# Two parameter loads in place of a small weight read on ScalarE's DMA queue

## The chip, the cores and the metric

The kernel runs on one core of a Trainium2 chip. The metric is the device time of one execution in microseconds (us). Of seven runs of the kernel before, the median is 180.34 us, the lowest 180.09 and the highest 180.94. The engines of the core are named as in the profile: PE (matrix multiplication, with PEld for its weight loads), DVE (vector engine), ACT (ScalarE, activations), POOL (GpSimd) and SP (which here only issues DMAs). ACT can issue DMAs, too; "ACTq" and "SPq" stand for the two issuing queues.

## The reference

The input is 2048 rows of 512 numbers. Each row is normalized; the normalized rows go through a diagonal complex state space model along the sequence and through a gated feed-forward network with a hidden width of 1376; both results are added to the input.

```python
xn = _layernorm(x, axis=-1)
return x + _A_ref(xn, ...) + _B_ref(xn, ...)

# _A_ref: state space model, 512 states
Lam = Lambda_re + 1j * Lambda_im
dt = jnp.exp(log_dt)
Lam_bar = jnp.exp(dt * Lam)
B_bar = ((Lam_bar - 1.0) / Lam)[:, None] * Bmat
Bu = jnp.einsum("bld,pd->blp", x + 0j, B_bar)
for t in range(L):
    h = Lam_bar[None, :] * h + Bu[:, t, :]
y = 2.0 * jnp.einsum("blp,dp->bld", hseq, Cmat).real + x * Dskip[None, None, :]

# _B_ref: gated network
return (silu(x @ w_gate) * (x @ w_up)) @ w_down
```

Inputs, weights and output are bfloat16.

## The kernel before

**Tiling.** The 2048 rows are 16 tiles of 128 rows (x0 to x15), in four chunks of four tiles. A chunk goes through these steps: layer norm of its tiles (statistics, L509, L527 or L479 on DVE; scale and shift into `xn_sb`), transposition of `xn_sb` into `xnT`, gate and up products (L739; for the first chunk the gate products are cut into quarters, L780), silu and copy out of PSUM on ACT (L751, L807), their product hT on DVE (L809), the state space input (L854, copied out at L861), rotation by tables, scan and rotation back on DVE (L885, L894), which leave `hss`, and the output product: `hT` with `w_down` (L937) and `hss` with `W12` (L950) into one PSUM bank, added to x on DVE (L955) and stored.

**PSUM.** Eight banks are used as four pairs. A product into a pair waits until ACT (or DVE at L955) has read what the pair held before. ACT writes the up products into two buffers `uf`, so the third waits for the hT that reads the first.

**What orders the work.** Each operation is a task with a list of tasks that it depends on and an estimated duration. PE and SP run their tasks in the order in which the code adds them. For ACT, DVE and POOL a planner (`_schedule`) walks through the estimated times and picks, among the tasks that are ready, the one with the longest estimated path behind it. For DMAs it works with an estimated bandwidth and latency of each queue. The order it makes is fixed when the kernel is built; on the chip, engines wait for each other by semaphores alone. An estimate that changes, also that of a load's arrival, can thus change the order of instructions on DVE far from the load.

**The head.** SP issues x0, x1, x2, a quarter of the first gate weights (`a2`, the last of four slices of 128 input rows), x3, three parameter loads, then the up weights, the rest of the gate weights and x4 to x7 as one load (`ld_x4`). ACT issues a small read `ld_touch` and the other three slices of the gate weights (`a0`: two slices, `a1`: one). `ld_touch` reads two numbers of each of four slices from every eighth row of the first 128 rows, into `tch`, which nothing reads. The gate weights' load `a0` keeps its place behind it through `order`. After its DMA issues ACT loads the table for Sqrt and runs one activation with it (`act_table`, L463). Then come the square roots of the first chunk (L521), each of which DVE's reciprocal (L531) waits for; the normalization (L514) follows that. PE first runs some matmuls on a constant (L474), then transposes the first normalized tiles (L565), which ACT copies out (L577).

**Parameters.** The three parameter vectors (log_dt, Lambda_im, Lambda_re) are loaded as rows of `prow`, transposed by PE (L562) together with the last tile of the first chunk and copied to `praw` (L574). From them small operations on 4 numbers per partition follow: `dt` and `r` on POOL (L636, L643), the range reductions and the complex factors on DVE (L610 to L660).

**The transposes on SP's queue.** After the head SP issues five transposing DMAs (L395): the two parts of B, `xnT` of chunk 1, and the two parts of C. Each waits for all DMAs added before it, and a plain load added after one waits for it. Behind them stand x8 to x11, `w_down` and x12 to x15. Chunk 2's statistics on DVE need x8 to x11; POOL makes `rstd` from them (L487, L491), DVE `nmr` (L500), and ACT normalizes the four tiles (L503), as it does for chunk 3.

**The scans.** A chunk has eight scans (L894), in two halves of four. A half needs its rotated input (L885) and carries a state to the next chunk.

Of the kernel before, what the change touches and what calls it, by code (L numbers as in the profile page):

```python
# [12 lines left out]
B16 = mybir.dt.bfloat16  # L13
# [236 lines left out]
def bass_parallel_sum__ssm_conv_s5__swiglu_ffn__prompt_kernel(  # L250
# [23 lines left out]
    KT = D // 128  # L274
# [6 lines left out]
    g = _Graph()  # L281
    es = ExitStack()
    with es:
        block = es.enter_context(nc.Block(no_gpsimd_drain=True))

        def sb(name, shape, dt):
            return es.enter_context(nc.sbuf_tensor(name, shape, dt))
# [41 lines left out]
        st0 = sb("st0", [128, 4, 2, 6], F32)  # L329
        sd0 = sb("sd0", [128, 4], F32)  # L330
        epst = sb("epst", [128, 1], F32)
        tch = sb("tch", [16, KT, 2], B16)
        praw = sb("praw", [128, 3, PT], B16)
        prow = sb("prow", [12, 128], B16)
        ecst = sb("ecst", [128, PT], F32)
# [1 line left out]
        NSM = 64  # L337
        sm = sb("sm", [128, NSM, PT], F32)
# [46 lines left out]
        wg_v = B_w_gate.rearrange("(k p) f -> p k f", p=128)  # L385
# [5 lines left out]
        def dma(name, dst, src, writes, nbytes, reads=(), after=(), out_=False, eng="sp", xpose=False, prio=0.0, order=(), **kw):  # L391
            after = tuple(after)
            if xpose:
                after = after + tuple(dma_tasks)
                fn = lambda e, dst=dst, src=src: e.dma_start_transpose(out=dst, in_=src)  # L395
                est, nb = 2000.0, int(nbytes * 1.2)
            else:
                if xp_state[0] is not None:
                    after = after + (xp_state[0],)
                fn = lambda e, dst=dst, src=src: e.dma_start(dst, src, **kw)  # L400
                est, nb = 330.0 + nbytes / 900.0, nbytes
            t = g.add(eng, fn, reads=reads, writes=writes, name=name, dma=True, after=after, out=out_, est=est, nbytes=nb, prio=prio, order=order)
            dma_tasks.append(t)
            if xpose:
                xp_state[0] = t
            return t
# [6 lines left out]
        def pload(name, slot, src, **kw):  # L413
            return dma(name, prow[4 * slot:4 * slot + 4, :], src.rearrange("(a p) -> a p", p=128), [("prow", slot)], 1024, **kw)

        def x_load(a, **kw):
            return dma("ld_x%d" % a, x_sb[:, a:a + 1, :], x_v[:, a:a + 1, :], [("x", a)], TILEB, **kw)

        def wg_load(nm, k0, k1, **kw):
            return dma("ld_wg" + nm, wg[:, k0:k1, 0:FG], wg_v[:, k0:k1, 0:FG], [("wg", nm)], (k1 - k0) * 128 * FG * 2, **kw)  # L420

        x_load(0)
        x_load(1)
        act_q = [dma("ld_touch", tch[0:16], wg_v[0:128:8, :, 0:2], [("tch",)], 16 * 16, eng="act")]
        act_q.append(wg_load("a0", 0, 2, eng="act", order=(act_q[-1],)))
        x_load(2)
        act_q.append(wg_load("a1", 2, 3, eng="act", order=(act_q[-1],)))
        wg_load("a2", 3, 4)
        x_load(3)
        pload("ld_ldt", 2, A_log_dt)  # L430
        pload("ld_lim", 1, A_Lambda_im)
        pload("ld_lre", 0, A_Lambda_re)
        dma("ld_wu0", wu[:, :, 0:FH0], wu_v[:, :, 0:FH0], [("wu", 0)], 512 * FH0 * 2)
        dma("ld_wg1", wg[:, :, FG:Fh], wg_v[:, :, FG:Fh], [("wg", 1)], 512 * (Fh - FG) * 2)
# [7 lines left out]
        def loads_stage_b2():  # L442
# [13 lines left out]
              reads=[("ones",)], writes=[("ident",)], name="ident", est=300)  # L456
        g.add("pool", lambda e: e.iota(iot[:], pattern=[[1, TP]], base=0, channel_multiplier=0, allow_small_or_imprecise_dtypes=True),
              writes=[("iot",)], name="iota", est=1000)
# [1 line left out]
        g.add("pool", lambda e: e.memset(car[:, 0], 0.0), writes=[("car", 0, 0), ("car", 0, 1)], name="car0", est=100)  # L460
        g.add("pool", lambda e: e.memset(ecst[:], math.e), writes=[("ecst",)], name="ecst", est=100)
        def act_table(func, order):
            g.add("act", lambda e: e.activation(out=sm[:, NSM - 1, 0:1], in_=epst[:], func=func, bias=epst[:, 0:1]), reads=[("epst",)], writes=[("sm", "_warm")],  # L463
                  name="act_warm", est=1500, order=order)

        act_table(AF.Sqrt, (act_q[-1],))

        def pe_warm(n, w=512, bk=None):
# [292 lines left out]
        def ffn_gate_quarters(pairs):  # L761
# [27 lines left out]
            for a_, b_ in zip(seq, seq[1:]):  # L789
                hold[b_].od.add(hold[a_])  # L790
            act_table(AF.Silu, (hold["ev21"],))
            hold["evac"] = g.tasks[-1]
            ffn_mm(0, NQ, "g", xt_pair[0])
# [275 lines left out]
```

## Time and profile before

| | |
|---|---|
| median of 7 runs | 180.34 us (180.09 to 180.94) |
| the profiled execution | 180.35 us |
| its span in the profile | 178.6 us |
| PE busy | 174.4 us (98%) |
| DVE busy | 162.2 us (91%) |
| ACT busy | 88.7 us (50%) |
| granted PE clock | 1.00 in the whole span |
| DMA | 12.37 MB, of it 11.54 MB on SP's queue and 0.69 MB on ACT's |

The span begins with the first instruction that the profile sees and ends with the last; the rest of the execution's time lies around it. PE's busy time has to be read with care, since matmuls are pipelined and overlap in the records: a row of the timeline that says 379 ns for a matmul stands for a new matmul every 216 ns. A timeline row gives start and duration in us, engine, line, operation, output and inputs; in brackets stands how long the engine had been idle before it and what ended that. In the chain of waits a row gives start, duration and what the end of the execution waited for in that stretch.

The landing times of the head's loads, from issue: x0 2.3 us, x1 3.0, x2 3.7, x3 4.3, `ld_touch` 2.1, a0 3.8, a1 4.3 and a2 4.4. The transposes land after 4.2 to 4.6 us, but that of chunk 1's `xnT` after 6.0.

### The profile page before, as it was taken

How to read it: one execution, taken by the hardware profiler on the slowest of the kernel's cores; microseconds unless marked ns; L12 is line 12 of the kernel's file. 1: busy time of each engine (PE TensorE's matmuls, PEld its weight loads, DVE VectorE, ACT ScalarE, POOL GpSimd, SP SyncE). 2: the span in 40 equal slices, each digit the busy share in tenths (PEclk: the TensorE clock that was granted, in tenths of full speed). 3: DMA queues.
4: the chain of work that ended last, by engine and by line, in shares of the span. 5: the costliest groups of instructions: out<-in, count | busy, mean ns of one | idle time of the engine just before them, and what ended most of it. 6: DMA issues, size and time to landing. Idle time of an engine off the chain costs nothing.

```text
span 178.6 us, 2429 instructions
## 1 busy us (share of the span) xinstructions
PE 174.4 (98%) x937; PEld 83.9 (47%) x937; DVE 162.2 (91%) x281; ACT 88.7 (50%) x114; POOL 9.5 (5%) x21
## 2 busy tenths in 40 slices
PE   8899999999999999999999999999999999999994
PEld 2794444444434444444444444444444444444743
DVE  2958984888899999999999999999999999999983
ACT  4469999999699957016565651000965620000000
POOL 3023200001300000040000000000000000000000
PEclk9999999999999999999999999999999999999999
DMA  5995563669360000002330000001100000000122
GB/s 165 386 319 119 117 121 43 129 174 352 118 117 4 0 0 0 0 6 86 84 65 0 0 0 4 0 0 59 59 0 4 0 0 0 0 0 4 59 88 89
DMA packets 22978, 12.37 MB, mean 69 GB/s; under 512 B 15192, under 2 KB 22968, under 8 KB 22968
## 3 DMA queue, kind: packets, MB, share of 16 engines
q1 hardware_dynamic: 22472, 11.54, 23.7%
q10 hardware_dynamic: 496, 0.69, 1.1%
q8 instruction: 7, 0.11, 0.3%
q14 instruction: 3, 0.02, 0.1%
HBM read 6.46 MB, written 2.10 MB: 48 GB/s over the span
## 4 chain that ended last, share of the span: by engine, by line
PE 94%; DMA 2%; ACT 2%; DVE 1%; issue 0%; SPq 0%
PE pb L739 34%; PE pb L937 21%; PE pb L950 16%; PE pb L854 15%; PE pb L780 4%; PE pb L817 2%; DMA x_sb<-in_A_x_dram 2%; PE pb L827 1%; PE pb L565 1%; ACT xn_sb L503 1%; ACT uf L807 1%; DVE st L509 0%; SPq L400 0%; ACT xnT L577 0%; DVE xn_sb L514 0%
## 5 line engine op out<-in xcount | busy, mean ns | idle before, releaser
L894 DVE TENSOR_TENSOR_SCAN rot<-sm,car,rot 128x512 bf16<-128x512 f32 x32 | 39.0, 1266 | 0.1
L937 PE MATMUL pb<-wd,hT 128*128 128x512 bf16 (+3 forms) x198 | 38.8, 355 | 0.0
L739 PE MATMUL pb<-xnT,wu 128*128 128x512 bf16 x160 | 37.3, 379 | 0.3 <-ACT uf L807 0.3
L739 PE MATMUL pb<-xnT,wg 128*128 128x512 bf16 x132 | 31.3, 379 | 0.0
L950 PE MATMUL pb<-W,hss 128*128 128x512 bf16 (+2 forms) x144 | 28.3, 355 | 0.0
L854 PE MATMUL pb<-xnT,BT 128*128 128x512 bf16 x128 | 28.1, 379 | 0.0
L937 PEld LDWEIGHTS pb<-wd,hT 128*128 128x128 bf16 (+1 forms) x198 | 18.5, 98 | 19.9
L739 PEld LDWEIGHTS pb<-xnT,wu 128*128 128x128 bf16 x160 | 15.5, 98 | 19.5 <-ACT uf L807 0.8
L751 ACT ACTIVATE sg<-pb 128x1024 bf16<-128x1024 f32 x20 | 20.1, 1025 | 8.5 <-PE pb L739 7.4
L807 ACT ACTIVATE uf<-pb 128x1024 bf16<-128x1024 f32 x20 | 20.6, 1028 | 6.8 <-PE pb L739 5.9
L950 PEld LDWEIGHTS pb<-W,hss 128*128 128x128 bf16 x144 | 13.5, 98 | 14.3
L739 PEld LDWEIGHTS pb<-xnT,wg 128*128 128x128 bf16 x132 | 12.7, 98 | 15.7 <-issue 0.8
L854 PEld LDWEIGHTS pb<-xnT,BT 128*128 128x128 bf16 x128 | 12.5, 98 | 15.1
L861 ACT ACTIVATE u_sb<-pb 128x1024 bf16<-128x1024 f32 x16 | 16.4, 1026 | 4.4 <-PE pb L854 4.1
L809 DVE TENSOR_TENSOR hT<-sg,uf 128x1024 bf16<-128x1024 bf16 x20 | 13.4, 680 | 1.1 <-ACT uf L807 1.0
L885 DVE TENSOR_TENSOR rot<-u_sb,cosT 128x2048 bf16<-128x2048 bf16 x8 | 9.7, 1217 | 2.8 <-ACT cosT L700 2.8
L955 DVE TENSOR_TENSOR x_sb<-pb,x_sb 128x512 bf16<-128x512 f32 (+2 forms) x18 | 10.9, 623 | 1.4 <-PE pb L950 1.4
L503 ACT ACTIVATE xn_sb<-x_sb,nmr,rstd 128x512 bf16<-128x512 bf16 x8 | 5.9, 804 | 9.9 <-DVE nmr L500 9.9
L836 ACT ACTIVATE sg<-pb 96x1024 bf16<-96x1024 f32 x2 | 2.0, 1019 | 17.3 <-PE pb L817 17.3
L885 DVE TENSOR_TENSOR rot<-rot,cosT 128x2048 bf16<-128x2048 bf16 x8 | 9.7, 1217 | 0.1
L885 DVE TENSOR_TENSOR rot<-rot,sin 128x2048 bf16<-128x2048 bf16 x8 | 9.7, 1218 | 0.0
L885 DVE TENSOR_TENSOR rot<-u_sb,sin 128x2048 bf16<-128x2048 bf16 x8 | 9.7, 1214 | 0.0
(78 smaller groups left out, 142.5 us busy)
## 6 DMA issues: line engine op xcount, KB each, us to landing
out_dram<-x_sb SPq DMA_DIRECT2D x15, 128.0 KB, 1.7
x_sb<-in_A_x_dram SPq DMA_DIRECT2D x3, 512.0 KB, 7.4
wd<-in_B_w_down_dram SPq DMA_DIRECT2D x1, 1280.0 KB, 6.9
wu<-in_B_w_up_dram SPq DMA_DIRECT2D x1, 768.0 KB, 4.8
wu<-in_B_w_up_dram SPq DMA_DIRECT2D x1, 608.0 KB, 7.0
x_sb<-in_A_x_dram SPq DMA_DIRECT2D x4, 128.0 KB, 3.4
wg<-in_B_w_gate_dram SPq DMA_DIRECT2D x1, 480.0 KB, 5.9
wg<-in_B_w_gate_dram ACTq DMA_DIRECT2D x1, 448.0 KB, 3.8
```

The source lines that it names most:

```text
L503: g.add("act", lambda e, a=a: e.activation(out=xn_sb[:, a % NXN, :], in_=x_sb[:, a, :], func=AF.Identity, scale=rstd[:, a:a + 1], bias=nmr ...
L739: inst = e.matmul(pbank[0:fs, bk, :].rearrange("p (j t) -> p j t", j=4), lhsT=w[:, kt, i * 128:i * 128 + fs], rhs=xnT[:, c % 2, :, kt, :], ...
L751: g.add("act", lambda e: e.activation(out=sg[rows, sl, 0:n, :].rearrange("p a t -> p (a t)"), in_=pair_f32(rows, bk, 512 * n), func=AF.Sil ...
L807: g.add("act", lambda e: e.activation(out=uf[rows, ul, 0:n, :].rearrange("p a t -> p (a t)"), in_=pair_f32(rows, bk, 512 * n), func=AF.Ide ...
L809: g.add("dve", lambda e: e.tensor_tensor(out=hT[rows, hb, i0:i0 + n, :], in0=sg[rows, sl, 0:n, :], in1=uf[rows, ul, 0:n, :], op=ALU.mult), ...
L854: inst = e.matmul(pbank[:, bk, :].rearrange("p (j t) -> p j t", j=4), lhsT=BT[:, ri, kt, pt * 128:(pt + 1) * 128], rhs=xnT[:, c % 2, :, kt ...
L861: g.add("act", lambda e: e.activation(out=u_sb[:, us].rearrange("p r t -> p (r t)"), in_=pair_f32(slice(0, 128), b0), func=AF.Identity), r ...
L885: tt = lambda out, a, b, op, r, w, nm: g.add("dve", lambda e: e.tensor_tensor(out=out, in0=a, in1=b, op=op), reads=r, writes=w, name="%s_% ...
L894: g.add("dve", lambda e, A0=A0, A1=A1, k=k, ri=ri, pt=pt: e.tensor_tensor_scan(out=A1[:, k, ri, :], data0=rr[:, pt:pt + 1].to_broadcast([1 ...
L937: inst = e.matmul(pbank[:, bk, 0:nc_], lhsT=hT[0:fs, hb, i, lt * 128:(lt + 1) * 128], rhs=wd[0:fs, i, c0:c0 + nc_], start=(i == 0), stop=F ...
L950: inst = e.matmul(pbank[:, bk, 0:nc_], lhsT=hss[:, hb, pt, ri, lt * 128:(lt + 1) * 128], rhs=W12[:, ri, pt, c0:c0 + nc_], start=False, sto ...
L955: g.add("dve", lambda e, bk=bk, a=a, c0=c0, nc_=nc_: e.tensor_tensor(out=x_sb[:, a, c0:c0 + nc_], in0=pbank[:, bk, 0:nc_], in1=x_sb[:, a, ...
```

## The change

On ACT's queue `ld_touch` and its tile `tch` go; the loads of log_dt and Lambda_im, which were on SP's queue, are issued there, in this order, ahead of a0. On SP's queue only Lambda_re is left of the three. The activation that comes with a table load loses its bias operand.

```diff
-        tch = sb("tch", [16, KT, 2], B16)
...
-        act_q = [dma("ld_touch", tch[0:16], wg_v[0:128:8, :, 0:2], [("tch",)], 16 * 16, eng="act")]
+        act_q = [pload("ld_ldt", 2, A_log_dt, eng="act")]
+        act_q.append(pload("ld_lim", 1, A_Lambda_im, eng="act", order=(act_q[-1],)))
         act_q.append(wg_load("a0", 0, 2, eng="act", order=(act_q[-1],)))
         x_load(2)
         act_q.append(wg_load("a1", 2, 3, eng="act", order=(act_q[-1],)))
         wg_load("a2", 3, 4)
         x_load(3)
-        pload("ld_ldt", 2, A_log_dt)
-        pload("ld_lim", 1, A_Lambda_im)
         pload("ld_lre", 0, A_Lambda_re)
...
-            g.add("act", lambda e: e.activation(out=sm[:, NSM - 1, 0:1], in_=epst[:], func=func, bias=epst[:, 0:1]), reads=[("epst",)], writes=[("sm", "_warm")],
+            g.add("act", lambda e: e.activation(out=sm[:, NSM - 1, 0:1], in_=epst[:], func=func), reads=[("epst",)], writes=[("sm", "_warm")],
```

As built, PE and POOL have the same instructions in the same order as before, and ACT's order differs only in its DMA issues. DVE's order differs in three places, shown here as built, other rows left out:

```diff
 L574 TensorCopy praw<-pb 128x12
-L651 TensorCopy sm<-praw 128x4 x2
-L610 TensorTensor sm<-sm 128x4 x3
-L660 Reciprocal sm<-sm 128x4
 L479 BNStats st<-x_sb 128x6 x4
 L483 BNStatsAggregate mv<-st 128x2 x4
...
 L622 TensorScalarPtr sm<-sm 128x4
+L651 TensorCopy sm<-praw 128x4 x2
+L610 TensorTensor sm<-sm 128x4 x3
+L660 Reciprocal sm<-sm 128x4
...
 L885 TensorTensor rot<-rot 128x2048
-L894 TensorScalarPtr rot<-sm,car,rot 128x512
 L479 BNStats st<-x_sb 128x6 x4
...
 L894 TensorScalarPtr rot<-sm,car,rot 128x512
 L500 TensorScalarPtr nmr<-mv,rstd 128x4
+L894 TensorScalarPtr rot<-sm,car,rot 128x512
 L843 TensorTensor hT<-sg,uf 96x2x512
...
 L903 TensorCopy ctmp<-rot 128x2x2
-L955 TensorTensor x_sb<-pb,x_sb 128x512
+L885 TensorTensor rot<-u_sb,cosT 128x2048
+L955 TensorTensor x_sb<-pb,x_sb 128x512 x2
 L500 TensorScalarPtr nmr<-mv,rstd 128x4
-L885 TensorTensor rot<-u_sb,cosT 128x2048
-L955 TensorTensor x_sb<-pb,x_sb 128x512
 L885 TensorTensor rot<-u_sb,sin 128x2048
```

In the first of these places the four normalizations of tiles 4 to 7 (L495) also stand ahead of the first hT (L809) instead of behind it. Line numbers are those of the kernel before; in the changed kernel lines from 332 on are one lower, and from 463 on two lower.

## The prediction

> **What bounds the kernel now.** I read the chain of waits first. It says 94% PE; in order of time PE runs from 6.44 us to 176.27 us with one stop. Then I read the end of the chain, and the timelines of DVE and of SP's queue for what sets that stop and how close DVE is behind PE.
>
> ```profile
> 48.12 1.41 ACT xn_sb L503 x2
> 49.53 0.92 ACT uf L807
> 50.45 0.05 issue
> 50.49 8.81 PE pb L739 x40
> ...
> 159.73 9.58 PE pb L937 x66
> 169.30 6.96 PE pb L950 x48
> ```
>
> The stop: L739 starts at 50.49 us, after 0.33 us of idle PE, because ACT normalized four tiles (L503) before it emptied the PSUM pair that PE wanted (L807). ACT had waited for nmr (L500) on DVE, and nmr goes back to a load:
>
> ```profile
> 38.23 1.28 DVE L894 TENSOR_TENSOR_SCAN rot<-sm,car,rot 128x512 bf16<-128x512 f32 x1
> 40.94 2.47 DVE L479 BATCH_NORM_STATS2 st<-x_sb 128x6 f32<-128x512 bf16 x4 [1.42 <-DMA x_sb<-in_A_x_dram]
> ...
> 46.32 0.16 DVE L500 SCALAR_TENSOR_TENSOR nmr<-mv,rstd 128x4 f32<-128x4 f32 x1 [0.86 <-POOL rstd L491]
> 46.40 0.68 DVE L843 TENSOR_TENSOR hT<-sg,uf 96x1024 bf16<-96x1024 bf16 x1
> 47.00 2.45 DVE L894 TENSOR_TENSOR_SCAN rot<-sm,car,rot 128x512 bf16<-128x512 f32 x2
> ...
> 79.64 0.16 DVE L500 SCALAR_TENSOR_TENSOR nmr<-mv,rstd 128x4 f32<-128x4 f32 x1 [0.26 <-POOL rstd L491]
> ...
> 166.28 2.36 DVE L885 TENSOR_TENSOR hss<-rot 128x2048 bf16<-128x2048 bf16 x2
> ```
>
> Note the brackets (idle time before the row and what ended it): 1.42 us until x tiles 8 to 11 landed, 0.86 us on POOL, 0.26 us at 79.64. After that the DVE rows follow each other without an idle bracket up to 170.94. The last row writes the last hss, which ends at 168.64; the first weight load of the matmuls that read it (L950) is at 169.08 in the weight-load timeline. With a hop of 0.05 (L807 ends 50.44, PE starts 50.49) DVE has 169.08 - 168.64 - 0.05 = 0.39 us in hand there. So two chains run to the end: PE's, pinned at 50.49, and DVE's, pinned at 40.94, only 0.39 us shorter. Both hang on one transfer, issued here:
>
> ```profile
> 13.83 2.29 SPq L395 DMA_TRANSPOSE BT<-in_A_B_re_dram  x1
> 18.17 2.07 SPq L395 DMA_TRANSPOSE BT<-in_A_B_im_dram  x1
> 22.52 1.80 SPq L395 DMA_TRANSPOSE xnT<-xn_sb  x1
> 28.55 1.97 SPq L395 DMA_TRANSPOSE hss<-in_A_C_re_dram  x1
> 33.17 1.86 SPq L395 DMA_TRANSPOSE hss<-in_A_C_im_dram  x1
> 37.42 0.37 SPq L400 DMA_DIRECT2D x_sb<-in_A_x_dram  x1
> ```
>
> Each waits for the one before to land; the first waits for all loads of the head, the last of which is x4 to 7 (DVE waited for it until 13.61).
>
> **The change, part by part.**
>
> SP's queue loses the rows log_dt (3.13 us) and Lambda_im (3.55); Lambda_re stood at 3.85. So that load and the four behind it are issued 3.85 - 3.13 = 0.72 us earlier. Does x4 land earlier? The windows table says what limits it:
>
> ```profile
> 11.50:12.00 0.50, 0.50 (x10) 0.38 (x7) 0.00 (x0) 0.49 (x2) 0.00 (x0) 1.00 1.10 368
> 12.00:12.50 0.50, 0.50 (x12) 0.50 (x10) 0.35 (x2) 0.14 (x1) 0.27 (x1) 1.00 1.11 352
> ```
>
> The next to last column is the DMA engines' share: it is 0.99 or more in every half microsecond from 3.0 to 13.0. The engines set the landing, not the issue, and the bytes are the same but for 64 four-byte packets. Bounds: 0.72 us earlier if issue decided after all; 0.30 us later if the engines lost all of the time by which the first gate weights are issued later (next part). I take 0: before 3.0 us ScalarE's queue moved 15.4% in 2.4 to 3.0, so 0.30 us of it is 0.05, and the removed packets (9.1% of 0.4 us) give 0.04 back.
>
> ScalarE's queue: log_dt (0.38 by SP's row) takes the place of the weight read (0.41), and Lambda_im adds SP's spacing 3.85 - 3.55 = 0.30. So a0 and a1 are issued at 1.53 and 2.02 instead of 1.23 and 1.72, and all behind them on ACT moves: table load 2.23 to 2.53, warm activation 3.53 to 3.83, ending at 4.12. The first Sqrt (sd0) started at 4.02 on mv; it may start some 0.1 late and end at 4.4. Its reader, the reciprocal L531, starts at 4.65, held by the half statistics of tile 1 (L509 at 4.31, x1 landing at 4.29), so 0.2 us of cover is left. a0 lands 1.23 + 3.8 = 5.03, would land 5.33, and is wanted at 6.44; a1 at 6.3 for 7.33. x1 may even land earlier, since a0 shared the engines with its last packets (ScalarE's queue has 83 to 97% of the engines from 3.0 to 4.2, SP's 7 to 18%); then sd0 is next, so the gain ends near 4.65 - 4.45 = 0.20. Head: -0.20 to +0.10. It costs or gives nothing at the end, because PE only reaches the stop at 50.16 earlier or later and starts again at 50.49 all the same; without that cover it would count whole.
>
> [...]
>
> Bounds for a0 without the read ahead, by the rows: the read took 2.1 us to land and a0 3.8. If a0 now paid those 2.1 us on top, it would land at 5.33 + 2.1 = 7.4, 1.0 us late, of which the stop hides 0.33: a loss of 0.7 us at most. At the other end it lands as before after its issue. I take 0, since the parameter loads, too, come ahead of it on that queue, and 1.1 us is in hand.
>
> The removed bias of the warm activation changes one operand, no instruction. POOL and PE keep their order.
>
> DVE's order changes. In the order as built, the six parameter operations (two casts, three multiplies, reciprocal; 12.54 to 13.40, 0.85 us) move from ahead of the statistics of tiles 4 to 7 to behind them. They lay under the wait for x4, so DVE now idles and does them after 17.0. xn4 to 7 (L495) now stand ahead of the first hT: 17.0 + 0.85 + 0.1 = 17.95, ending 19.24; hT 17.87 becomes 19.24. Behind the late hT waits uf of 19.82 on ACT (two buffers), now 19.9; ACT then had 0.33 us of idle before 21.48. DVE's 2.81 us of idle before 31.78 hides the rest. Cost 0.
>
> The scan at 38.23 moves behind nmr. Before it filled the wait for the load; now that wait is longer and the scan comes at 46.40, ahead of L843. One scan by spacing: (64.94 - 60.09)/4 = 1.21 and 9.42/8 = 1.18 (150.00 to 159.42), say 1.19. Queued behind it is all of DVE: L843 47.59, the two scans 48.19, hT at 51.8 and so on. Who waits: the uf activations (54.18 on ACT needs 52.4: free), PE's first L950 (75.30 needs W at 73.73 + 1.19 = 74.92: 0.38 left). At 79.64 the second nmr is also moved, behind a 1.13 us product and one addition; so POOL's rstd is ready in time and the gap there (78.70 + 0.60 = 79.30 to 79.64) closes: 0.34 given back, at the price of ACT's L503 at 82.4 and its first silu at 85.3 instead of 84.39, taken up by ACT's 0.70 gaps. What remains is 1.19 - 0.34 = 0.85, and with no idle row it reaches 166.28. The last hss is then done at 168.64 + 0.85 = 169.49, its weights load at 169.54 instead of 169.08: PE stops 0.46 us, and the additions and stores behind it end as much later.
>
> Sum, against the profiled execution (180.35 us; its span 178.6 and 1.75 around it; the runs' median is 180.34): 180.35 + 0.46 = 180.8.
>
> **The rivals.** Let e be how much earlier x8 to 11 land. PE can come at most 0.33 (the stop) plus 0.20 (head) earlier; DVE's end moves by 0.46 - e. The change is the larger of -min(e, 0.53) and 0.46 - e.
>
> Faster: the transpose at 22.52 took 6.0 us where the other two of its line took 4.3. Its last packets lie behind one instruction read of 0.02 MB at 26.3 to 27.0. If they escape it, e = 1.7, the stop goes, the late scan costs nothing: 180.35 - 0.53 = 179.8. It decides from e = 0.46 on, where the change is nothing; from e = 0.82 on the gain is over 0.36. For it: the collision is by a hair. Against: the read follows PE's place, and a PE that is earlier meets more of the transfer.
>
> No difference: e of 0.1 to 0.8, from the 0.72 us of issue time, or a DVE chain with idle too small to be shown: at e = 0.72 it is 180.35 - 0.26 = 180.1, at 0.46 it is 180.35. Against it stands the DMA share.
>
> Slower still: x4 lands 0.30 later and all of the transposes with it; both pins move, 180.8 + 0.3 = 181.1. Or a0 is late by the bound of 0.7 past the stop; then PE, not DVE, sets the end: 180.35 + 0.7 = 181.05. For it: a0 and its queue are the only loads that the change delays. Against: a0 has 1.1 us in hand (5.33 against 6.44).
>
> That the change does not do what it says is no rival here: each engine's order is fixed when the kernel is built.
>
> **How the numbers follow.** Forecast (180.6 to 181.0) 0.52, faster 0.25, no difference 0.13, slower still 0.10. A change of 0.2% is 0.36 us, about what a measurement of this kernel can tell from none. Of the forecast's 0.52 some 0.07 falls under 180.70, so slower 0.45 + 0.10 = 0.55, same 0.20, faster 0.25. The range reaches from the faster case (179.8, a little under) to just past slower still: 179.75 to 181.2; the forecast's own range is 180.6 to 181.0.
>
> **What would show it.** Right: DVE's statistics of tiles 8 to 11 start near 40.9 after about 2.6 us of idle, a scan directly behind nmr, no idle at the second nmr, and an idle PE of near 0.46 us released by DVE before the last L950. Wrong: the gap between the third and fourth transpose near 4.3 us instead of 6.0, a first transpose more than 0.3 us from 13.83, idle DVE rows between 47 and 166, or first L780 matmuls that wait for wg.

## The result, and the profile after

| | before | changed |
|---|---|---|
| median | 180.28 us (179.80 to 180.99, 31 runs) | 181.51 us (181.02 to 182.12, 12 runs) |
| ratio, 95% interval | | 1.0068 [1.0055, 1.0081] |
| profiled execution (span) | 180.35 us (178.6) | 181.44 us (179.7) |
| PE, DVE, ACT busy | 174.4, 162.2, 88.7 us | 175.0, 161.6, 87.8 us |

The change makes the kernel slower by 0.68%, or some 1.2 us; between the two profiled executions it is 1.1 us. The forecast was slower by 0.46 us. The granted clock is 1.00 in both. Line numbers of the changed kernel are one or two lower than before (L477 is L479 before, L892 is L894, L948 is L950).

The chain of waits of the changed kernel, which was 94% PE before (start, duration, what the end waited for):

```profile
by line: DVE rot L883 23.5%; DVE rot L892 20.5%; DMA x_sb<-in_A_x_dram 7.3%; DVE hT L807 6.0%; DVE hss L883 5.1%; DVE st L477 4.1%; PE pb L948 4.0%; DVE x_sb L953 3.3%; DMA xnT<-xn_sb 3.2%; DMA hss<-in_A_C_im_dram 2.4%; DMA hss<-in_A_C_re_d
...
23.54 5.72 DMA xnT<-xn_sb
29.29 4.20 DMA hss<-in_A_C_re_dram
33.51 4.36 DMA hss<-in_A_C_im_dram
37.88 3.65 DMA x_sb<-in_A_x_dram
41.55 2.48 DVE st L477 x4
45.05 1.87 POOL rstd L489
47.17 1.20 DVE rot L892
...
167.91 2.28 DVE hss L883 x2
170.24 7.13 PE pb L948 x48
```

The end now hangs on DVE, from the landing of x8 to 11 (37.88 + 3.65 us) to the last `hss`; PE has only the last row. The timelines of PE, DVE and SP's queue of the changed kernel give the sizes:

```profile
51.15 1.04 PE L737 MATMUL pb<-xnT,wu 128*128 128x512 bf16 x4 [1.22 <-ACT uf L805]
...
170.24 5.14 PE L948 MATMUL pb<-W,hss 128*128 128x512 bf16 x23 [0.28 <-DVE hss L883]
...
41.55 2.48 DVE L477 BATCH_NORM_STATS2 st<-x_sb 128x6 f32<-128x512 bf16 x4 [3.60 <-DMA x_sb<-in_A_x_dram]
...
47.01 0.16 DVE L498 SCALAR_TENSOR_TENSOR nmr<-mv,rstd 128x4 f32<-128x4 f32 x1 [0.93 <-POOL rstd L489]
47.09 1.28 DVE L892 TENSOR_TENSOR_SCAN rot<-sm,car,rot 128x512 bf16<-128x512 f32 x1
...
82.92 0.15 DVE L498 SCALAR_TENSOR_TENSOR nmr<-mv,rstd 128x4 f32<-128x4 f32 x1
...
167.83 2.34 DVE L883 TENSOR_TENSOR hss<-rot 128x2048 bf16<-128x2048 bf16 x2
...
14.88 1.97 SPq L394 DMA_TRANSPOSE BT<-in_A_B_re_dram  x1
...
37.88 0.37 SPq L399 DMA_DIRECT2D x_sb<-in_A_x_dram  x1
```

Against the rows shown of before: the first transpose is issued 1.05 us later (13.83, now 14.88). On the way the transposes give back more than half: x8 to 11 are issued 0.46 later (37.42, 37.88). They land 0.61 later (L477 starts at 41.55 instead of 40.94), `nmr` comes 0.69 later (46.32, 47.01) and the last `hss` 1.55 later (166.28, 167.83). PE, which reached its stop earlier than before (51.15 - 1.22 = 49.93, before 50.16), goes on 0.66 later (50.49, 51.15), and a second stop, 0.28 us of shown idle, has come at the last L948.

Why the first transpose is late shows in part in the windows table. The last three columns are granted clock, the DMA engines' busy share and GB/s. First the changed kernel:

```profile
2.50:3.00 0.50, 0.50 (x3) 0.22 (x2) 0.00 (x0) 0.33 (x1) 0.00 (x0) 1.00 1.20 288
3.00:3.50 0.50, 0.50 (x3) 0.21 (x2) 0.49 (x1) 0.50 (x1) 0.00 (x0) 1.00 0.79 83
3.50:4.00 0.50, 0.50 (x3) 0.15 (x1) 0.47 (x3) 0.49 (x2) 0.00 (x0) 1.00 0.71 242
...
6.50:7.00 0.50, 0.50 (x13) 0.50 (x10) 0.47 (x3) 0.20 (x1) 0.00 (x0) 1.00 1.06 251
7.00:7.50 0.50, 0.50 (x13) 0.50 (x10) 0.50 (x3) 0.29 (x2) 0.00 (x0) 1.00 0.86 273
7.50:8.00 0.50, 0.50 (x13) 0.50 (x10) 0.42 (x2) 0.28 (x2) 0.00 (x0) 1.00 0.98 338
```

and the same stretches of the kernel before:

```profile
2.50:3.00 0.50, 0.50 (x3) 0.22 (x2) 0.00 (x0) 0.50 (x1) 0.00 (x0) 1.00 0.74 169
3.00:3.50 0.50, 0.50 (x3) 0.21 (x2) 0.42 (x1) 0.50 (x1) 0.00 (x0) 1.00 1.01 287
3.50:4.00 0.50, 0.50 (x3) 0.15 (x1) 0.45 (x2) 0.31 (x2) 0.00 (x0) 1.00 1.02 383
...
6.50:7.00 0.50, 0.50 (x12) 0.50 (x10) 0.50 (x2) 0.36 (x1) 0.00 (x0) 1.00 1.06 395
7.00:7.50 0.50, 0.50 (x12) 0.50 (x10) 0.47 (x4) 0.13 (x1) 0.00 (x0) 1.00 1.06 393
7.50:8.00 0.50, 0.50 (x13) 0.50 (x10) 0.44 (x3) 0.44 (x2) 0.00 (x0) 1.00 1.08 406
```

There are two dips. The one at 3.0 to 4.0 us loses (287 - 83 + 383 - 242) x 0.5 us = 172 KB, the one at 6.5 to 8.0 loses (395 - 251 + 393 - 273 + 406 - 338) x 0.5 us = 166 KB; at some 390 GB/s these are 0.44 and 0.43 us. Other stretches give part of it back. From 2.5 to 3.0 the changed kernel moves more than before (288 against 169 GB/s), so that by 4.0 us it is 124 KB behind in all, 0.32 us at the same rate; it gains again after 8.0 us, and at 13.0 it is 209 KB behind, 0.54 us. The rest of the 1.05 lies in the end of these loads, which thins out: 297, 115 and 14 GB/s in the three half microseconds from 13.0 to 14.5, where before only the first still moved anything, at 12 GB/s. Why it does is not shown. In the row 6.50:7.00 the engines are as busy as before (1.06) and move 251 GB/s instead of 395: the busy share is no measure of what is moved.

### The profile page after: what moved, and what is told of

Read it like the earlier page. It is cut to its first block, busy times and chain, and to the rows that moved or that the text cites. A ratio compares the mean times of both kernels' runs of the same rounds, so it can differ in the third digit from the quotient of the medians.

```text
span 179.7 us, 2428 instructions
## 1 busy us (share of the span) xinstructions
PE 175.0 (97%) x937; PEld 84.1 (47%) x937; DVE 161.6 (90%) x281; ACT 87.8 (49%) x114; POOL 10.7 (6%) x21
## 4 chain that ended last, share of the span: by engine, by line
DVE 74%; DMA 15%; PE 4%; SPq 2%; POOL 1%; issue 1%; DVEq 0%
DVE rot L883 24%; DVE rot L892 20%; DMA x_sb<-in_A_x_dram 7%; DVE hT L807 6%; DVE hss L883 5%; DVE st L477 4%; PE pb L948 4%; DVE x_sb L953 3%; DMA xnT<-xn_sb 3%; DMA hss<-in_A_C_im_dram 2%; DMA hss<-in_A_C_re_dram 2%; SPq L399 2%; DVE xn_sb L587 2%; DVE W L712 1%; DVE W L709 1%; DVE x_sb L589 1%
## 5 line engine op out<-in xcount | busy, mean ns | idle before, releaser
L892 DVE TENSOR_TENSOR_SCAN rot<-sm,car,rot 128x512 bf16<-128x512 f32 x32 | 39.0, 1266 | 0.0
L948 PE MATMUL pb<-W,hss 128*128 128x512 bf16 (+2 forms) x144 | 28.3, 355 | 0.3 <-DVE hss L883 0.3
L948 PEld LDWEIGHTS pb<-W,hss 128*128 128x128 bf16 x144 | 13.4, 98 | 14.7 <-DVE hss L883 0.5
L477 DVE BATCH_NORM_STATS2 st<-x_sb 128x6 f32<-128x512 bf16 x12 | 7.4, 682 | 6.0 <-DMA x_sb<-in_A_x_dram 6.0
```

Source lines behind the costliest of these rows:

```text
L477: return g.add("dve", lambda e, a=a: e.bn_stats(out=st[:, a, :], in_=x_sb[:, a, :]), reads=[("x", a)], writes=[("st", a)], name="bnst%d" % ...
L892: g.add("dve", lambda e, A0=A0, A1=A1, k=k, ri=ri, pt=pt: e.tensor_tensor_scan(out=A1[:, k, ri, :], data0=rr[:, pt:pt + 1].to_broadcast([1 ...
L948: inst = e.matmul(pbank[:, bk, 0:nc_], lhsT=hss[:, hb, pt, ri, lt * 128:(lt + 1) * 128], rhs=W12[:, ri, pt, c0:c0 + nc_], start=False, sto ...
```

## The experiments

The planner's order depends on the loads, so in most experiments the order of DVE and ACT was given by lists taken from the kernel before or from the changed one:

```diff
+        for eng_, order_ in (("dve", DVE_ORDER), ("act", ACT_ORDER)):
+            ts_ = [t for t in g.tasks if t.eng == eng_ and not t.dma]
+            streams[eng_] = [t for t in streams[eng_] if t.dma] + [ts_[i] for i in order_]
```

"Order before" and "changed order" mean these lists; ACT's list is the same in both. The kernel before was measured beside each group, with medians of 180.75, 180.51 and 180.50 us, so ratios are compared, not times.

**The two halves of the change.** First only the order: the kernel before and its loads, with the changed order on DVE.

> The loads of the kernel before, with DVE's order of the changed kernel. If the order costs what the prediction said (one scan, less the gap at the second nmr, less 0.39 us in hand), the end is 0.4 to 0.5 us later: 180.7 us, a stop of PE of about 0.45 us before the last L950, first transpose near 13.8 us. If the order costs nothing by itself and only late transfers do: 180.3 us.

Measured: ratio 1.0020 [1.0005, 1.0036]. Its timelines of PE and DVE:

```profile
50.67 1.90 PE L741 MATMUL pb<-xnT,wu 128*128 128x512 bf16 x8 [0.50 <-ACT uf L809]
169.70 5.57 PE L952 MATMUL pb<-W,hss 128*128 128x512 bf16 x26 [0.22 <-DVE hss L887]
...
41.11 2.47 DVE L481 BATCH_NORM_STATS2 st<-x_sb 128x6 f32<-128x512 bf16 x4 [2.91 <-DMA x_sb<-in_A_x_dram]
...
46.50 0.16 DVE L502 SCALAR_TENSOR_TENSOR nmr<-mv,rstd 128x4 f32<-128x4 f32 x1 [0.87 <-POOL rstd L493]
...
167.30 2.35 DVE L887 TENSOR_TENSOR hss<-rot 128x2048 bf16<-128x2048 bf16 x2
```

The second stop is there without any change of the loads, released by DVE's last `hss`. From `nmr` to the last `hss` DVE takes 167.30 - 46.50 = 120.80 us, before 166.28 - 46.32 = 119.96: the order adds 0.84, where the prediction said 0.85. The loss, 0.0020 x 180.75 = 0.36 us (0.09 to 0.65 by its interval), is close to the forecast's 0.46 for this part.

Then only the loads: the changed kernel with the order before.

> The loads of the changed kernel, with DVE's order of the kernel before. If the loads alone move the transposes, the first of them starts near 14.9 us, x8 to 11 land 0.6 us later, the stop ends near 51.1 and the time is 0.6 to 0.7 us above before: 180.95 us, with no stop before the last L950. If the order is all: 180.3 us.

Measured: 1.0018 [1.0003, 1.0034]. Its windows and its only stop of PE:

```profile
3.00:3.50 0.50, 0.50 (x3) 0.21 (x2) 0.50 (x1) 0.50 (x1) 0.00 (x0) 1.00 0.95 95
3.50:4.00 0.50, 0.50 (x3) 0.15 (x1) 0.47 (x3) 0.49 (x2) 0.00 (x0) 1.00 0.64 191
...
50.85 1.90 PE L739 MATMUL pb<-xnT,wu 128*128 128x512 bf16 x8 [0.64 <-ACT uf L807]
```

The first dip comes with the loads, the second does not (380, 341 and 387 GB/s from 6.5 to 8.0), and the first transpose starts at 14.49. x8 to 11 land 0.32 later than before (DVE's statistics at 41.26), PE goes on 0.36 later, and no stop follows at the end. So each half costs about 0.2%, and one does it through DVE's end, the other through PE's stop.

**The changed kernel once more**, beside the second group.

> The changed kernel once more, beside the others on one chip: if its loss is the sum of late loads (0.33 us measured alone) and late scan (0.36 us measured alone), 0.7 us above before; if the two add to more, 1.2 us as in the first measurement.

Measured: 1.0070 [1.0045, 1.0096], with both dips (117 GB/s in 3.0 to 3.5, 264 in 7.0 to 7.5) and both stops (2.00 at 52.10, 0.25 at 171.16). The whole measures more than the two halves (0.20% + 0.18%). Taken with the first measurement, 0.68%, the surplus is 0.30%, just clear of an uncertainty of 0.26% that the three intervals give together; with this second one alone it would not be. In the profiles the difference is the second dip, which neither half shows, and a chunk-1 transpose of 6.33 us.

**Is it the missing read ahead?** The changed kernel with the small read put back ahead of the two parameter loads, changed order.

```diff
-        act_q = [pload("ld_ldt", 2, A_log_dt, eng="act")]
+        act_q = [dma("ld_touch", tch[0:16], wg_v[0:128:8, :, 0:2], [("tch",)], 16 * 16, eng="act")]
+        act_q.append(pload("ld_ldt", 2, A_log_dt, eng="act", order=(act_q[-1],)))
```

> The changed kernel with the small read of the gate weights put back ahead of the two parameter loads on ACT's queue, DVE's order of the changed kernel. Theory of the read ahead: the slow first packets of the gate weights go, x4 to 7 land near 13.6 us again and only the order is left to pay: 180.7 us. Theory of the queues (parameter loads ahead of a0 on ACT's queue and earlier issue on SP's spoil the transfers): x4 to 7 land at 14.6 us or later: 181.5 us.

Measured: 1.0089 [1.0057, 1.0121], no better than without it (1.0068 and 1.0070). a0 is issued at 2.13 us, the dip lasts to 4.5 (157, 195, 190 GB/s), and x8 to 11 land at 42.41. The theory of the read ahead falls: with the read, the dip stays. But a0 is issued later still here, so this run alone does not part the read from the time of issue; the next three do.

**Is it the read alone that matters?** The kernel before without the small read, parameters on SP, order before.

```diff
-        act_q = [dma("ld_touch", tch[0:16], wg_v[0:128:8, :, 0:2], [("tch",)], 16 * 16, eng="act")]
-        act_q.append(wg_load("a0", 0, 2, eng="act", order=(act_q[-1],)))
+        act_q = [wg_load("a0", 0, 2, eng="act")]
```

> The kernel before without the small read; parameter loads stay on SP's queue, DVE's order of before. Theory of the read ahead: first packets of a0 take some 0.25 us each as in the changed kernel, x4 to 7 land about 1 us later, 180.95 us. Theory of the queues: as before or a little faster, since a0 is issued 0.44 us earlier: 180.0 to 180.3 us.

Measured: 1.0046 [1.0026, 1.0067]. There is no dip (375, 390 GB/s), but with a0 issued at 0.79, beside x0, the first x tiles land later: the first statistics, of x0, start at 3.48 us instead of 3.08, those of x1 at 5.03 instead of 4.31. PE is idle ahead of its first transposes, and its first gate products then run at half speed:

```profile
5.96 0.40 PE L565 MATMUL pb<-ident,xn_sb 128*128 128x128 bf16 x2 [0.92 <-DVE xn_sb L514]
...
7.02 1.70 PE L780 MATMUL pb<-xnT,wg 128*128 128x128 bf16 x14
8.51 0.42 PE L565 MATMUL pb<-ident,xn_sb 128*128 128x128 bf16 x2
8.72 1.40 PE L780 MATMUL pb<-xnT,wg 128*128 128x128 bf16 x14
```

From 7.02 to 8.72 these are 16 matmuls, 14 gate products and two transposes, 106 ns each. In the kernel before the same 16 take 6.28 to 7.17, 56 ns each:

```profile
6.28 0.94 PE L780 MATMUL pb<-xnT,wg 128*128 128x128 bf16 x14
...
7.17 0.94 PE L780 MATMUL pb<-xnT,wg 128*128 128x128 bf16 x14
```

So the small read has a use: with it a0 is issued at 1.23 instead of 0.79, and the statistics of x0 and x1 start 0.40 and 0.72 us earlier. In these runs the weights came too early as well as too late: a0 at 0.79 went with 0.46% more time, a0 at 1.67, in the kernel with the loads only, with 0.18%.

**What makes the dip?** Two kernels with the order before. In the first a second small read, of other rows, delays a0, and the parameters stay on SP. In the second one parameter load takes the small read's place.

```diff
+        act_q.append(dma("ld_touch2", tch2[0:16], wg_v[4:128:8, :, 0:2], [("tch2",)], 16 * 16, eng="act", order=(act_q[-1],)))
```

> The kernel before with a second small read of the gate weights (16 rows, 64 packets) between the first and a0, so that a0 is issued near 1.67 us as in the changed kernel, but with no parameter load ahead of it; parameters on SP's queue, DVE's order of before. If the later issue of a0 makes the slow packets from 3.0 to 3.75 us: the same dip (below 200 GB/s there), x4 to 7 near 14.3 us, time 0.3 us above before. If it is the parameter loads ahead of a0: no dip, x4 to 7 near 13.7 us, time as before.

```diff
-        act_q = [dma("ld_touch", tch[0:16], wg_v[0:128:8, :, 0:2], [("tch",)], 16 * 16, eng="act")]
+        act_q = [pload("ld_ldt", 2, A_log_dt, eng="act")]
...
-        pload("ld_ldt", 2, A_log_dt)
```

> The kernel before with log_dt in the place of the small read (a0 issued near 1.4 us, close to the 1.23 of before), the other parameters on SP's queue, DVE's order of before. If a parameter load ahead of a0 makes the slow packets by its form (4 rows, 4 packets): a dip below 200 GB/s between 2.7 and 3.75 us, x4 to 7 near 14.1 us. If the time of a0's issue does: hardly a dip, x4 to 7 near 13.7 us, time as before.

Measured: 1.0018 [0.9999, 1.0037] and 1.0020 [1.0001, 1.0039]. The times do not tell the two apart, the transfers do. The issue of a0 on ScalarE's queue and the windows, first of the kernel with two small reads:

```profile
1.71 0.97 ACTq L403 DMA_DIRECT2D wg<-in_B_w_gate_dram  x2
...
3.00:3.50 0.50, 0.50 (x3) 0.21 (x2) 0.39 (x1) 0.50 (x1) 0.00 (x0) 1.00 0.80 154
```

then of the one with one parameter load:

```profile
1.38 0.92 ACTq L401 DMA_DIRECT2D wg<-in_B_w_gate_dram  x2
...
3.00:3.50 0.50, 0.50 (x3) 0.21 (x2) 0.46 (x1) 0.50 (x1) 0.00 (x0) 1.00 0.98 281
```

The first has no parameter load on ScalarE's queue and dips; the second has one and does not. What goes with the dip is the time at which a0 is issued: 1.66 us and later dips at 3.0 to 3.5, 1.38 and earlier does not, in all profiles of this case. What the dip costs is not shown by this pair: the kernel without it is as slow as the one with it, and its first transpose starts at 14.20, against 14.31 with the dip and 13.83 before.

**The parameter loads behind the weights**: small read, a0 and a1 as before, then the two parameter loads on ScalarE's queue, order before.

```diff
         act_q.append(wg_load("a1", 2, 3, eng="act", order=(act_q[-1],)))
+        act_q.append(pload("ld_ldt", 2, A_log_dt, eng="act", order=(act_q[-1],)))
+        act_q.append(pload("ld_lim", 1, A_Lambda_im, eng="act", order=(act_q[-1],)))
```

> The kernel before with log_dt and Lambda_im on ACT's queue, but behind a0 and a1, the small read ahead of a0 kept; DVE's order of before. If the parameter loads spoil the transfers only by standing ahead of a0: no dip from 3.0 to 3.75 us and x4 to 7 near 13.6 us or earlier, time as before (the table load comes 0.7 us later, of which 0.2 us in the head have cover and 0.33 us the stop hides: 0 to 0.2 us more). If any parameter load on ACT's queue, or the earlier issue on SP's queue, is enough: x4 to 7 at 14.3 us, time 0.3 us above before.

Measured: 1.0053 [1.0034, 1.0072], a median of 181.39 us over six runs. There is no dip (352, 382 GB/s), but ACT's table load moves to 3.15 and its first Sqrt to 4.65, so that the first normalized tile is late. The profiled execution, with 180.25 us the lowest of the six, has no stop at 50 and does not show what the others lost; of this kernel only the transfers are read.

**Is it a0's place behind x2?** The changed kernel with x2 issued behind a2 on SP's queue, changed order.

```diff
-        x_load(2)
         act_q.append(wg_load("a1", 2, 3, eng="act", order=(act_q[-1],)))
         wg_load("a2", 3, 4)
+        x_load(2)
```

> The changed kernel with x2 issued behind the last slice of the first gate weights instead of ahead of it, changed order on DVE. Theory A (the slow first transfers between 3 and 4 us come from the first gate weights being issued after x2, whose transfer then comes first on the engines): the dip (83 GB/s in 3.0 to 3.5) goes, to 280 GB/s or more, the first transpose starts near 13.9 instead of 14.88 and the time falls to about 180.8 (the late scan alone is left), unless x2 itself is late for its statistics and costs the head 0.2 us or more. Theory B (they come from the time of issue alone, 1.67 us and later): the dip stays, the first transpose stays at 14.5 or later, the time near 181.5.

Measured: 1.0053 [1.0030, 1.0076]. The dip stays, deeper (72 and 118 GB/s), so theory A falls. x2 lands late as the expectation allowed: its statistics start at 7.55 after 1.83 us of idle, and PE stops 1.03 us in the head, which sets the end here. Why a late a0 starts slowly stays open.

**Does everything hang on x8 to 11?** Both kernels with the load of x8 to 11 issued ahead of the two transposes of C, each with its own DVE order.

```diff
+            dma("ld_x8", x_sb[:, 8:12, :], x_v[:, 8:12, :], [("x", a) for a in range(8, 12)], 4 * TILEB)
...
-            dma("ld_x8", x_sb[:, 8:12, :], x_v[:, 8:12, :], [("x", a) for a in range(8, 12)], 4 * TILEB)
```

> The kernel before, with the load of x8 to 11 issued ahead of the two transposes of C instead of behind them, engine orders as before. Theory (the end hangs on the landing of x8 to 11, by two chains): the statistics of tiles 8 to 11 have no DMA wait any more (it was 1.42 us), the stop of PE near 50.5 (0.33) goes, and the time falls by 0.33 us to about 180.0. Rival (the two transposes of C, now later by one load of about 4 us, become the next thing that is late, or PE loses in the stage at another place): the stop goes but the time does not fall, 180.3 or more.

> The changed kernel with the same early load of x8 to 11, with the changed order on DVE. Theory (the whole loss of about 1.2 us is the late landing of x8 to 11, once through PE's stop near 51 and once through the late scan): both PE's stop near 51 (1.22) and the one before the last output product (0.28) go, and the time is that of the kernel before with the same early load, within 0.3 us, near 180.0 or below, since PE had reached its stop 0.23 us earlier in the changed kernel (49.93 against 50.16). Rival (part of the loss is in the head, in the slower first transfers themselves): it stays 0.5 us or more above its counterpart.

Measured: 0.9966 [0.9949, 0.9982] for the kernel before, 0.9959 [0.9942, 0.9977] for the changed one (179.79 and 179.76 us). For the kernel before that is 0.61 us, where 0.33 was forecast; in its profile 0.22 us more is there at the first gate product already (6.06 against 6.28), and counts now that no stop follows. The second kernel, from its windows, its DVE timeline and the chain on its page:

```profile
3.00:3.50 0.50, 0.50 (x3) 0.22 (x2) 0.50 (x1) 0.50 (x1) 0.00 (x0) 1.00 0.72 132
3.50:4.00 0.50, 0.50 (x3) 0.15 (x1) 0.47 (x3) 0.49 (x2) 0.00 (x0) 1.00 0.85 270
...
37.75 2.47 DVE L479 BATCH_NORM_STATS2 st<-x_sb 128x6 f32<-128x512 bf16 x4
...
164.82 2.35 DVE L885 TENSOR_TENSOR hss<-rot 128x2048 bf16<-128x2048 bf16 x2
...
PE 96%; ACT 1%; ACTq 1%; DVE 0%; issue 0%
```

The first dip and the late scan are still there, the statistics wait for no DMA, no stop of PE is left after 45 us, and the loss of 0.68% is gone. This settles the path: neither the first dip nor the late scan costs time once x8 to 11 land early.

Last, the kernel before with the early load and the planner's own order.

> The kernel before with the early load of x8 to 11, with the planner's own orders, which that earlier landing changes on DVE and ACT. Theory (the landing decides): no stop of PE near 50.5, about 180.0. Rival (the new order brings a wait of its own, as the changed kernel's order did): a stop of PE between 50 and the end with another releaser than the normalization of tiles 8 to 11, 180.3 or more.

Measured: 0.9970 [0.9952, 0.9988]. The new order brings no stop. Three kernels thus beat the kernel before by 0.3 to 0.4%, and the changed one by more; their intervals do not tell them apart.

## Why the prediction was right and wrong

**The direction and the late scan: right.** The step "0.85 lag less 0.39 in hand" held: `nmr` is 0.69 late, the last `hss` 1.55, so 0.86 was added in between (0.84 with the order alone), and the gap at the second `nmr` closed (no bracket at 82.92). The order alone measured 0.36 us where the step said 0.46.

**The step that failed** is the landing of x4 to 7: "I take 0", with a bound of 0.30 us on the late side. DVE's wait for it ended at 14.72 us instead of 13.61, and the first transpose was issued 1.05 us late, of which 0.61 reached the landing of x8 to 11 and moved both chains, PE's by 0.66 and DVE's by 0.69. The sum with the measured term is 0.46 + 0.66 = 1.12, against 1.1 between the profiles. The mechanism is that of the rival "slower still"; its 0.30 was too small. Two readings led there. A busy share of 0.99 was taken for full transfer, but 0.95 goes with 95 GB/s in the kernel with the loads only. And the 0 took a0's delay at the 15.4% that ScalarE's queue moved before 3.0 us, 0.05 us, where by 4.0 us the transfers were 0.32 us behind. That is near the bound, whose own base was short: it took log_dt's issue at SP's 0.38 us, but on ScalarE it lasts 0.55, and a0 came at 1.67, 0.44 later and not 0.30. No term stood for the second dip and for the thin end of the loads. The kernel with the loads only, which has no second dip, shows 0.32 of the 0.61 at the landing of x8 to 11; what brings the rest stays open.

**The head: right.** The first gate product starts at 6.12 instead of 6.28, and PE reached its stop 0.23 earlier, just past the bound of 0.20, which gave nothing, as said. a0 was in time: no gate product waits for it. The six parameter operations cost nothing: PE has no idle bracket between 8 and 49.9 us.

**The faster rival did not happen.** The chunk-1 transpose did not escape the instruction reads: it took 5.72 us, against 6.03 before, with two reads in it. That the read follows PE's place is seen later in the execution: the last four of the seven larger reads come behind 451, 579, 707 and 834 recorded matmuls in both profiles. In this transpose the larger read came behind 196 matmuls, at 24.50 us, where before it came behind 204, at 26.50.

## What to carry to other kernels

Read the GB/s column beside the busy share before a transfer is called limited by its engines (a share of 1.06 stood beside 251 GB/s and beside 395); small DMAs ahead of a large one on the same queue set when the large one is issued (a0 at 0.79 us with none, at 1.23 with one read, at 1.67 with two parameter loads), and the first and the last of these were both slower here (by 0.46%, and with the loads only by 0.18%). Where an engine's order is made from estimates, a moved load changes work far away, and order and loads are to be costed and tested apart. When two chains hang on one landing, bring that landing forward first: here one moved line was worth 0.34%, and made the other losses vanish.

## What the runs showed of the hardware

**A late first weight load goes with slow transfers at 3 us.** In the seven profiles in which a0 is issued at 1.66 us or later the engines move 72 to 157 GB/s from 3.0 to 3.5; in the seven in which it is issued between 0.79 and 1.38 they move 232 to 375. Part of this may be a slow stretch that only comes later: from 2.5 to 3.0 the five profiles with a0 at 1.23 or 1.24 move 98 to 230 GB/s, those with a late a0 247 to 288. From 1.5 to 4.0 us together the seven late ones move 377 to 473 KB and the seven early ones 541 to 592, so the later issue costs even so. The cause is not known.

These bytes alone do not set when the first transpose starts. It starts at 14.31 to 14.90 in the late profiles and at 13.83 to 14.58 in the early ones; the 14.58 belongs to the kernel before with the early load of x8 to 11, whose loads up to there are those of the kernel before. With the same loads it thus starts anywhere from 13.83 to 14.58 in the four profiles that have them; their mean is 14.08, and 14.67 in the four profiles with the loads of the changed kernel. The 1.05 us between the two profiles read above is more than this 0.59. The second dip of the changed kernel was seen in both of its profiles, strongly in no other, not even in the changed kernel with the early load of x8 to 11, which is the same up to that load (344, 344 and 366 GB/s from 6.5 to 8.0); it is not explained either.

**The chunk-1 transpose stops for a while behind instruction reads.** The changed kernel's windows in the chunk-1 transpose (23.54 to 29.29):

```profile
25.00:25.50 0.50, 0.50 (x4) 0.22 (x3) 0.50 (x3) 0.50 (x3) 0.00 (x0) 1.00 3.11 155
25.50:26.00 0.50, 0.50 (x4) 0.20 (x2) 0.50 (x2) 0.50 (x2) 0.00 (x0) 1.00 0.43 6
26.00:26.50 0.50, 0.50 (x4) 0.26 (x3) 0.47 (x3) 0.50 (x2) 0.00 (x0) 1.00 0.08 10
```

By the lists of queues, cut into quarters of a microsecond, an instruction read of 0.02 MB falls between 24.50 and 24.75 and one of 0.01 MB between 26.75 and 27.00. Some 0.75 us behind each the transfer all but stops, for 1.0 us at 25.5 and for 0.5 us at 27.5. The transpose took 4.63 and 4.67 us in the kernels without the small read and with the parameters behind the weights, where one read falls behind nearly all of its packets, and 6.33 with two reads in the changed kernel's second profile. The reads are not all of it: the kernel before, too, has its one read behind nearly all packets, but two more packets come some half a microsecond or more behind it, and it took 6.03. That the reads cause the gaps is read from this order in time and was not tested by itself.

**Half speed that the clock column does not show.** The 106 ns per matmul of the kernel without a small read stand beside a granted clock of 1.00, and so do the 56 ns of the kernel before (both from 7.0 to 8.5 us). From 10.07 to 10.97 the kernel without a small read has 16 more, at 56 ns each. What halves the speed before that is not shown.
